# Linear attention and a gated MLP in one kernel: three x sums and two row sums earlier on VectorE, P V one slot sooner

## The chip, the cores and the metric

One NeuronCore of one Trainium2 chip. The time is the device time of one execution in microseconds (us); lower is better.

## The reference

Eight batches of 8 heads, 1024 positions, head size 64. Keys and values are first projected along the sequence to 64 rows, so attention has 64 columns:

```python
k_proj = np.einsum('ks,bhsd->bhkd', E, k)
v_proj = np.einsum('ks,bhsd->bhkd', F, v)
scores = np.matmul(q, k_proj.transpose(0, 1, 3, 2)) / np.sqrt(64)
attn = softmax(scores)                      # over 64 columns
x = concat_heads(np.matmul(attn, v_proj))   # 8192 x 512
out = (silu(x @ w_gate) * (x @ w_val)) @ w_out   # 512 -> 1536 -> 512
```

## The kernel before

**Chunks, tiles, slots.** The 8192 rows are 16 chunks `c` of 512 (batch `b` has chunks 2b and 2b+1, its halves `ch` 0 and 1). The MLP of a chunk runs over 12 tiles `f` of 128 hidden columns, so there are 192 tiles in a row. Each tile `t` is issued in a fixed order: `f_g` (gate matmuls), slot 2t, `f_v` (value matmuls), the tile's "late" list, slot 2t+1. The slots hold the attention of the next batch, so attention and MLP share all engines. `place(b)` puts the steps of batch b's attention in slots counted from `s0 = 48 * (b - 1)`, the first slot of batch b-1's MLP. Slots s0 to s0+23 therefore lie in an even chunk, and s0+24 to s0+47 in an odd one; s0+16 and s0+17 are the two slots of tile 8 of the even chunk, s0+43 and s0+44 the last of tile 9 and the first of tile 10 of the odd one. The order is written out by hand: each engine takes its instructions in the order in which the code issues them, and waits on semaphores for the others.

**Attention steps.** `u_S`: eight score matmuls for two groups (L378), exponential on ACT (L386). `u_R`: row sum and reciprocal on DVE (L408, L409). `u_N`: product with the reciprocal on POOL (L423) and a small running sum `zsum` on POOL (L439). `u_AD`: transposes the products by a DMA. `u_PVt`: eight matmuls of P V into four PSUM banks (L482) and four copies on ACT into `xT` (L491), the MLP's input. The banks are named by letters: `a` (two buffers), `g` (two, shared with the gate's output), `v` (two), `y` and `z` (one each, shared with the output matmuls).

**Pairs of value tiles.** In chunks after the first few, the value product of the tile pairs (2,3), (5,6) and (9,10) is made from seven half-size products instead of eight. For that, sums of blocks of `xT` are needed: `p_x(c, m)` makes them on DVE (L612), for m = 4, 3, 1 and "67", before the pair at tile 2 reads them. They are kept apart for even and odd chunks. `p_34` (first tile of the pair) makes products 4 and 3; `p_1` follows in the same tile's late list; `p_52` is at the second tile, and `p_76` after `f_g` of the tile after the pair. `p_34` takes the next buffer of `v` for its result and holds the other, that of the last `f_v`, for `p_1`; `p_76` adds to a bank that DVE must first have read for `p_52` (`sx`, L632). All matmuls of these have line 621. `gate` (L570) multiplies gate and value into `hT` on DVE; each tile's result waits there until its late list has passed `f_m` and `p_1`.

**The output product** `f_m(c, n)` of a chunk runs in the tiles of the next one, as seven half-size products too (L769). Its inputs `hs` are sums of blocks of `hT`: for m = 5 and 2 on POOL in 12 small steps (`h_sum`, L752, in the late lists of tiles 7, 8 and 11 and of tile 0 of the next chunk), the others on DVE. `f_m` needs m = 5 in tile 2 and m = 2 in tile 3. `m_16` and `m_7` combine the results: L798 and L804 on DVE with L799 on POOL between them. `m_52` copies bank `y` on ACT (L793).

**Late list, chunks after the third.** It is sorted: `f_m` and `p_1` first, then `gate`, then the sums:

```python
todo.sort(key=lambda x: (x[0] not in (f_m, p_1)) * 2)
todo.insert(sum(x[0] in (f_m, p_1) for x in todo), (gate,))
```

Of the kernel before, what the change touches and what calls it, by code (L numbers as in the profile page):

```python
# [26 lines left out]
NFT = DFF // P  # L27
# [16 lines left out]
def kernel(  # L44
# [822 lines left out]
    def put(s, fn, *a):  # L867
        slots[s].append((fn, a))

    def place(b):  # L870
        s0 = 48 * (b - 1)
        if b == 1:
            put(22, u_TD, 1, 0)
            put(29, u_K1, 1)
            put(32, u_KT, 1)
            put(40, u_V1, 1)
            sa = (35, 36, 37, 38, 41, 42, 43, 44)
            put(41, u_AD, 1, 0)
            put(30, u_TD, 1, 1)
            put(47, u_AD, 1, 1)  # L880
            put(46, u_PVt, 1, 0, (0, 1), ("aa", "av"))
        else:
            if b == 2:
                put(s0 + 10, u_KV, b)
            else:
                put(s0 + 8, u_KV, b, "kv", (0, H), "v")
            put(s0 + (13 if b == 2 else 10), u_KT, b)
            put(s0 + (9 if b == 2 else -6), u_TD, b, 0)
            put(s0 + (11 if b == 2 else -4), u_TD, b, 1)
            sa = [s0 + j for j in ((15, 15, 17, 17) if b == 2 else (13, 13, 15, 15)) + (23, 23, 25, 25)]  # L890
            put(s0 + 29, u_AD, b, 0)
            put(s0 + 44, u_AD, b, 1)
            put(s0 + 44, u_PVt, b, 0, (0, 1), ("aa", "yz"))
        for j in range(NJ):
            put(sa[j], u_S, b, j)
            at = sa[j] + 1 if b == 1 else s0 + (
                17, 17 + 2 * (b == 2), 21 if b == 2 else 19, 23 if b == 2 else 21, 35, 37, 41, 42)[j]
            put(at, u_R, b, j)
            put(at, u_N, b, j)
        put(s0 + (68 if b == 1 else 56), u_PVt, b, 1, (0, 1), ("aa", "yz"))  # L900
# [52 lines left out]
    with tc.manual_schedule():  # L953
# [132 lines left out]
        for b in range(1, B):  # L1086
            place(b)
        for b in range(2, B):
            s0 = 48 * (b - 1) - (20 if b == 3 else 24)
# [33 lines left out]
                late[t].append((p_w, m, p))  # L1123
        for c in range(3, NC):
            for i, m in enumerate((4, 3, 1, 67)):
                t = c * NFT + ((-1, -1, 0, 0) if c == 3 else (-3, -3, 0, 1) if c % 2 else (0, 0, 1, 2))[i]
                late[t].append((p_x, c, m))
        for p, cs in PAIRED.items():
            for c in cs:
# [4 lines left out]
        for t in range(NIT):  # L1134
            c, f = divmod(t, NFT)
            ring["wide"] = c < 2
            i = 1 if t < 2 else None
# [46 lines left out]
```

## Time and profile before

| | |
|---|---|
| median of 3 runs | 553.2 us (553.13 to 554.39) |
| profiled execution | 552.91 us, of it a span of 551.4 us from first to last instruction |
| TensorE clock granted | 0.998 of full speed |
| busy, of the span | PE 96%, DVE 78%, POOL 61%, ACT 52% |
| DMA | 62.94 MB, mean 114 GB/s |

PE is TensorE, DVE VectorE, ACT ScalarE, POOL GpSimd; SP issues DMAs. A row of the timeline gives the start in us, the duration, the engine, the line, the operation, what it writes and reads, how many instructions were merged into the row (x4), and in brackets how long the engine had been idle before it and which instruction ended that. A row of the waits gives the waiting engine and line, the one waited for, the total in us, how often, and the longest. A few matmul records are missing, so a group of four may be shown as x3.

### The profile page before, as it was taken

The numbers are of one execution on the slowest core, as the hardware profiler recorded it, in microseconds if no ns is written. First come the engines' busy times: TensorE is split into PE (matmuls) and PEld (weight loads), VectorE is DVE, ScalarE is ACT, GpSimd is POOL, SyncE is SP. The second block draws the span as 40 slices with busy tenths as digits, with TensorE's granted clock in tenths as the row PEclk, the third lists the DMA queues.
The fourth block names the chain that finished last, engine by engine and source line by source line (L and its number), as shares of the span: only waits on it lengthen the run. The fifth ranks groups of instructions, "written<-read, shape, count | busy, mean of one in ns | idle before, by whom it ended". The sixth has DMA issues, their size and how long they took to land.

```text
span 551.4 us, 9977 instructions
## 1 busy us (share of the span) xinstructions
PE 530.6 (96%) x3715; PEld 334.9 (61%) x3780; DVE 431.7 (78%) x724; ACT 288.0 (52%) x515; POOL 333.8 (61%) x428
## 2 busy tenths in 40 slices
PE   8999999999999999999999899998999989999996
PEld 4654545556666666666666666575665756566665
DVE  3787896687788996889887887879978789686874
ACT  3564454573457635566546564566444763453431
POOL 6962494376745957177761878448574574734562
PEclk9999999999999999999999999999999999999999
DMA  9999969829921697009941099314990121200013
GB/s 199 191 196 190 175 142 184 168 76 149 210 63 40 129 214 154 6 36 191 191 115 39 27 196 189 89 39 82 188 198 31 39 77 39 77 35 16 28 40 117
DMA packets 112228, 62.94 MB, mean 114 GB/s; under 512 B 65968, under 2 KB 103856, under 8 KB 112176
## 3 DMA queue, kind: packets, MB, share of 16 engines
q0 software_dynamic: 43952, 29.49, 37.4%
q1 hardware_dynamic: 67392, 31.46, 22.8%
q10 hardware_dynamic: 832, 1.31, 0.8%
q8 instruction: 30, 0.49, 0.3%
q14 instruction: 22, 0.18, 0.1%
HBM read 60.29 MB, written 16.78 MB: 140 GB/s over the span
## 4 chain that ended last, share of the span: by engine, by line
PE 76%; DVE 8%; ACT 6%; POOL 5%; issue 3%; DMA 2%; ACTq 0%; POOLq 0%; DVEq 0%
PE gps L536 23%; PE yps L769 20%; PE vps L536 16%; PE vps L621 9%; DMA wv<-in_moe_w_val_dram 2%; PE kvp L187 2%; PE sc L378 2%; PE yps L703 2%; DVE zr L408 2%; ACT ee L386 2%; POOL AAd L423 1%; POOL hs L752 1%; DVE xsa L612 1%; DVE hT L570 1%; DVE ts L652 1%
## 5 line engine op out<-in xcount | busy, mean ns | idle before, releaser
L536 PE MATMUL gps<-xT,wg 128*128 128x512 bf16 (+1 forms) x729 | 190.9, 377 | 1.7
L752 POOL TENSOR_TENSOR hs<-hT 128x256 bf16<-128x256 bf16 x180 | 130.3, 754 | 29.4 <-DVE hT L570 26.4
L536 PE MATMUL vps<-xT,wv 128*128 128x512 bf16 (+1 forms) x460 | 119.4, 376 | 1.7 <-DMA wv<-in_moe_w_val_dram 0.8
L536 PEld LDWEIGHTS <-wg 128*128 128x128 bf16 x776 | 74.3, 98 | 51.8 <-issue 0.5
L769 PEld LDWEIGHTS <-hs 128*128 128x128 bf16 x900 | 87.5, 98 | 24.7 <-issue 3.1
L799 POOL TENSOR_TENSOR tt<-tt,ysb 128x512 f32<-128x512 f32 x28 | 41.7, 1490 | 85.1 <-DVE tt L798 85.1
L562 ACT ACTIVATE th<-gps 128x512 f32<-128x512 f32 x82 | 49.0, 598 | 78.8 <-PE gps L536 76.0
L423 POOL TENSOR_TENSOR AAd<-ee,zr 128x512 bf16<-128x512 f32 x56 | 59.5, 1062 | 37.1 <-ACT ee L386 17.8
L536 PEld LDWEIGHTS <-wv 128*128 128x128 bf16 x480 | 45.5, 98 | 48.4 <-issue 4.0
L570 DVE TENSOR_TENSOR hT<-th,vps 128x512 bf16<-128x512 f32 x82 | 55.2, 682 | 22.6 <-ACT th L562 13.5
L769 PE MATMUL yps<-ws,hs 128*128 128x256 bf16 x540 | 68.6, 272 | 1.0 <-DVE ysb L838 0.2
L570 DVE TENSOR_TENSOR hT<-thp,sx 128x512 bf16<-128x512 f32 x74 | 58.3, 787 | 3.2 <-DVE sx L632 0.5
L632 DVE TENSOR_TENSOR sx<-ts,vps 128x512 f32<-128x512 f32 x74 | 49.5, 669 | 12.3 <-PE vps L621 10.9
L649 ACT COPY sx<-vps 128x512 f32<-128x512 f32 x37 | 21.7, 586 | 64.6 <-PE vps L621 64.6
L788 POOL TENSOR_TENSOR tt<-xs 128x256 f32<-128x256 f32 x30 | 25.7, 856 | 46.7 <-ACT xs L786 46.5
L769 PE MATMUL yps<-wo,hs 128*128 128x256 bf16 x360 | 48.8, 273 | 0.4 <-ACT xs L786 0.4
L769 PE MATMUL yps<-ws,hT 128*128 128x256 bf16 x360 | 48.8, 273 | 0.4
L752 DVE TENSOR_TENSOR hs<-hT 128x1536 bf16<-128x1536 bf16 (+1 forms) x49 | 46.6, 979 | 0.1
L408 DVE TENSOR_REDUCE zr<-ee 128x8 f32<-128x512 f32 x64 | 42.7, 667 | 3.1 <-ACT ee L386 3.1
L769 PEld LDWEIGHTS <-hT 128*128 128x128 bf16 x360 | 35.2, 98 | 13.2
L612 DVE TENSOR_TENSOR xsa<-xT 128x512 bf16<-128x512 bf16 (+1 forms) x39 | 38.6, 993 | 0.0
L386 ACT ACTIVATE ee<-sc 128x512 f32<-128x512 f32 x64 | 35.5, 597 | 5.3 <-PE sc L378 2.9
(134 smaller groups left out, 729.2 us busy)
## 6 DMA issues: line engine op xcount, KB each, us to landing
out_dram<-ysb SPq DMA_DIRECT2D x27, 512.0 KB, 3.0
qb<-in_q_dram POOLq DMA_DIRECT2D x14, 512.0 KB, 15.4
kb<-in_k_dram POOLq DMA_DIRECT2D x7, 1024.0 KB, 9.7
vb<-in_v_dram POOLq DMA_DIRECT2D x7, 1024.0 KB, 11.4
wo<-in_moe_w_out_dram POOLq DMA_DIRECT2D x2, 768.0 KB, 21.5
out_dram<-ysb SPq DMA_DIRECT2D x6, 256.0 KB, 2.7
kraw<-in_k_dram ACTq DMA_DIRECT2D x2, 512.0 KB, 4.7
qb<-in_q_dram POOLq DMA_DIRECT2D x4, 256.0 KB, 7.9
```

Of the source, the lines that this page charges most:

```text
L386: nc.scalar.activation(out=e[:].rearrange("p h j k -> p (h j k)"), in_=ps[:].rearrange("p a k -> p (a k)"), func=AF.Exp, scale=scale,)
L408: nc.vector.reduce_sum(out=z, in_=e[:], axis=AX.X)
L423: eng.tensor_tensor(out=a.rearrange("p j h k -> p h j k"), in0=ee.pop((b, u))[:], in1=r.unsqueeze(3).to_broadcast([P, 4, 2, KP]), op=ALU.mult,
L536: nc.tensor.matmul(out=ps[:, ts], lhsT=(wg, wv)[w][:, kt, f * P : (f + 1) * P], rhs=x[:, kt, ts], start=(kt == 0), stop=(kt == NKT - 1),)
L562: nc.scalar.activation(out=th[:], in_=ps[:], func=AF.Silu)
L570: nc.vector.tensor_tensor(out=h, in0=th, in1=v, op=ALU.mult)
L612: nc.vector.tensor_tensor(out=sums["x", m, c % 2], in0=i0, in1=i1, op=op)
L621: nc.tensor.matmul(out=ps, lhsT=w[:, kt], rhs=xs[:, kt], start=(start and kt == 0), stop=(kt == 1), skip_group_check=True,)
L632: nc.vector.tensor_tensor(out=out, in0=a.unsqueeze(1).to_broadcast([P, 2, HT]), in1=b, op=op)
L752: eng.tensor_tensor(out=hs[c, m][:, fs, :], in0=quarter(hT[c], *a)[:, fs], in1=quarter(hT[c], *b)[:, fs], op=op,)
L769: nc.tensor.matmul(out=ps, lhsT=lhsT, rhs=ws[m][:, f, :] if rhs is None else rhs, start=(start and f == 0), stop=(f == HF - 1), skip_group ...
L799: nc.gpsimd.tensor_tensor(out=t[:], in0=t[:], in1=yo[c, p][:, 1:3], op=ALU.subtract)
```

## The change

For batches after the second, the row sums and products of groups 0 and 1 go from slot s0+17 to s0+16, so they are issued before `f_v` of tile 8 and ahead of its `gate`. For odd chunks from the fifth on, the x sum m=4 is issued in tile 6 of the chunk before instead of tile 9, m=3 in tile 7 instead of 9, and m=1 in tile 11 of the chunk before instead of tile 0 of its own. P V of a batch's first half (batches from the second on) goes from slot s0+44 to s0+43, ahead of `f_g` of tile 10, and its third bank is a buffer of `g` where it was `y`.

```diff
-            put(s0 + 44, u_PVt, b, 0, (0, 1), ("aa", "yz"))
+            put(s0 + 43, u_PVt, b, 0, (0, 1), ("aa", "gz"))
...
             at = sa[j] + 1 if b == 1 else s0 + (
-                17, 17 + 2 * (b == 2), 21 if b == 2 else 19, 23 if b == 2 else 21, 35, 37, 41, 42)[j]
+                *((17, 19, 21, 23) if b == 2 else (16, 16, 19, 21)), 35, 37, 41, 42)[j]
             put(at, u_R, b, j)
             put(at, u_N, b, j)
...
             for i, m in enumerate((4, 3, 1, 67)):
-                t = c * NFT + ((-1, -1, 0, 0) if c == 3 else (-3, -3, 0, 1) if c % 2 else (0, 0, 1, 2))[i]
+                t = c * NFT + ((-1, -1, 0, 0) if c == 3 else (-6, -5, -1, 1) if c % 2 else (0, 0, 1, 2))[i]
                 late[t].append((p_x, c, m))
```

## The prediction

> **What bounds the kernel now.** I read the page first, then the waits of PE, then the timeline around the longest of them. The page says that PE is the bound and that little of it is idle:
>
> ```profile
> PE 530.6 (96%) x3715; PEld 334.9 (61%) x3780; DVE 431.7 (78%) x724; ACT 288.0 (52%) x515; POOL 333.8 (61%) x428
> ```
>
> The waits of PE, longest first; the second line is the start, and only the first repeats:
>
> ```profile
> PE vps L621 <- DVE sx L632: 7.1, 6, 1.5
> PE warm L992 <- DVE zeros L970: 1.4, 1, 1.4
> ```
>
> Where those waits stand: tiles 8 to 11 of chunk 8 (an even one), 303 to 317 us. To be seen: DVE idles 1.57 us before 305.26, then has no hole until PE waits at 311.62.
>
> ```profile
> 303.00 0.69 DVE L570 TENSOR_TENSOR hT<-thp,sx 128x512 bf16<-128x512 f32 x1
> 303.16 4.20 POOL L752 TENSOR_TENSOR hs<-hT 128x256 bf16<-128x256 bf16 x6
> 305.26 0.69 DVE L570 TENSOR_TENSOR hT<-th,vps 128x512 bf16<-128x512 f32 x1 [1.57 <-ACT th L562]
> 305.87 0.68 DVE L408 TENSOR_REDUCE zr<-ee 128x8 f32<-128x512 f32 x1
> 306.27 0.38 PE L621 MATMUL vps<-xsa,wo 128*128 128x256 bf16 x2
> 307.49 1.15 DVE L652 TENSOR_TENSOR ts<-sx 128x256 f32<-128x256 f32 x1
> 308.56 0.43 DVE L612 TENSOR_TENSOR x<-xT 128x512 bf16<-128x512 bf16 x1
> 308.92 1.26 DVE L612 TENSOR_TENSOR xsa<-xT 128x512 bf16<-128x512 bf16 x1
> 309.10 1.03 PE L536 MATMUL gps<-xT,wg 128*128 128x512 bf16 x3
> 310.93 0.64 DVE L632 TENSOR_TENSOR sx<-ts,vps 128x512 f32<-128x512 f32 x1
> 311.62 0.60 PE L621 MATMUL vps<-xsa,wo 128*128 128x256 bf16 x4 [1.49 <-DVE sx L632]
> 316.57 1.30 POOL L752 TENSOR_TENSOR hs<-hT 128x256 bf16<-128x256 bf16 x2 [0.60 <-DVE hT L570]
> ```
>
> The odd chunk that follows, tile 10 (338 to 342 us): P V, then p_52, then PE at L769 starts late.
>
> ```profile
> 338.63 0.59 ACT L793 COPY ysb<-yps 128x512 f32<-128x512 f32 x1
> 339.29 0.63 PE L482 MATMUL pv<-AT,VS 64*64 64x512 bf16 x8
> 339.39 0.60 ACT L555 ACTIVATE thp<-gps 128x512 f32<-128x512 f32 x1
> 339.85 0.61 PE L621 MATMUL vps<-xT,wo 128*128 128x256 bf16 x4
> 339.96 2.05 ACT L491 CAST xT<-pv 128x512 bf16<-128x512 f32 x4
> 340.60 1.47 PE L769 MATMUL yps<-ws,hs 128*128 128x256 bf16 x12
> ```
>
> A wait is counted from the modelled end of the last matmul, so I count loss by starts. Matmuls of 512 columns start 0.216 us apart and of 256 0.109 apart (the twelve of L769 from 307.79 to 309.10). So p_76 could start at 309.10 + 0.87 = 309.97 and starts at 311.62: **1.65 lost**. The chunks at 180, 377 and 443 us repeat it, the one at 245 loses 0.99 (due 244.49, starts 245.48). Together 7.6 us. At L769 of tile 10 the loss is 340.60 - (339.85 + 0.43) = **0.32**, in six odd chunks, 1.9 us. More than 9.5 us the change cannot take away by these two.
>
> **The change, part by part.** Nothing is added or dropped; instructions change places, no DMA is among them and SP's queue stays. The x sums move in six even chunks, 4 to 14; chunk 14 has no row sums and DVE is busy for 6.5 of 10 us there (500 to 510), so I count nothing for it.
>
> *A. The m=4 sum goes to tile 6.* On the timeline DVE idles 0.70 us before L688 (301.60, waiting for ACT). A sum alone takes 0.43 (308.56), POOL does not run until 302.41. Cost nothing; without that hole the sum would delay p_76 of the pair before by 0.43, and PE's next use of that bank, f_v of tile 8 at 302.80, is 1.6 us later.
>
> *B. The m=3 sum goes to tile 7, two row sums to slot 16.* They now stand on DVE ahead of the tile-8 product L570 (305.26), in the hole of 1.57 us. The sum starts at 303.61. POOL is in its first h_sum until 304.21; rows of L612 beside h_sums took 0.51 and 0.89, alone 0.43, beside the attention product L423 1.26. I take 0.89 (same neighbour, the start falls early in POOL's instruction): 304.50. The two row sums with reciprocals take 1.62 (305.87 to 307.49, L408 to L652). They need only exponentials done at 301.07. L570 starts at about 304.42 + 1.62 = 306.04 instead of 305.26 and ends at 306.73.
>
> The Trainium skill's "SBUF — State Buffer", in "Who interferes with whom", speaks against B: a VectorE instruction with two SBUF inputs and a GpSimd instruction that reads SBUF exclude each other for a whole instruction. By it the sum could take a whole h_sum, 0.67, plus 0.43, so 1.10 as an estimate, and the loss below would be 0.72; the rows of 0.43 to 1.26 agree in kind.
>
> *C. A new wait.* L570 of tile 8 empties the bank that p_1 of tile 9 overwrites (p_34 takes the other bank of v). p_1 starts at 306.27; L570 ended at 305.95, so it had 0.32 to spare. Now it can start at 306.73 + 0.05 (DVE end to PE start, 311.56 to 311.62) = 306.78: **0.51 lost**, and all of f_g(10), p_52, f_m and f_g(11) queue behind it. Bounds: sum of 0.43 gives 0.06, sum of 1.26 gives 0.88. In the chunk at 245 us L691 began 0.35 late, since POOL's L788 came first; there the loss is 0.85.
>
> *D. The p_76 wait goes.* After L570 come ts (0.49 to 1.15, by 307.9), one row sum (0.83, by 308.7) and sx, which needs p_52 (ends 307.96 + 0.51 = 308.5): done 309.4. p_76 is due at 309.97 + 0.51 = 310.48. Gain 1.65 - 0.51 = 1.14 in four chunks, 0.99 - 0.85 = 0.14 in the fifth.
>
> *E. What is late next: POOL.* Two attention products of 1.05 with their zsum (1.37 together) now stand ahead of four h_sums. POOL: first product at 305.4 when its reciprocal ends, second ends with zsum by 308.3, four h_sums (0.67) to 311.0, third product 312.4, L799 (1.27) 313.7, fourth product with zsum 315.2. On DVE L804 waits for L799, then two L570 of 0.69 to 0.91: h_sum f5 starts at about 315.75 instead of 316.57, so 0.8 earlier while PE is 1.14 earlier. The last h_sum that m=5 needs ended at 320.70, PE wanted it at 320.97 (matmuls from 320.53): 0.2 to spare. So 1.14 - 0.8 - 0.2 = 0.14 is given back, more if the m=1 sum, now beside these h_sums, holds up POOL by 0.38 (h_sums of 1.05 for 0.67). Bounds 0 and 0.6; I take **0.25** in four chunks. The m=1 sum at tile 11 is otherwise free (L688 has 0.47 idle before it).
>
> *F. P V a slot sooner, bank g for y.* PE's own order only swaps f_g(10) and P V: p_52 stays due at 339.85 and f_m at 340.28. ACT copies the z bank first; after L793 and L657 it is free at 339.50 and has copied z by 340.0. The 0.32 goes. New conditions: f_g(10) needs silu L651 of tile 9 (ends 338.74; f_g now starts 338.98), f_g(11) needs the g bank copied (340.5; 341.6). L555 now waits behind four copies and ends at 342.0 instead of 340.0; its reader, L570 at 342.52, comes later still. If that cover were gone, DVE would be late by at most 0.2. With y kept, P V would wait for L793 (ends 339.22) at 338.42, 0.8. In the sixth chunk (472 us) PE waits again at 475.09 for a chain through POOL's zsum, so I count five: 1.6 us.
>
> **Sum.** 4 x (1.14 - 0.25) + 0.14 + 1.6 = 5.3 us. The profiled execution took 552.91 (span 551.4 and 1.5 around it), so 547.6; the median of 553.2 stands 0.3 above it: **547.9**.
>
> **Rivals.** *The waits only move* (no gain by D). If the m=3 sum takes 1.26 and L691 is 0.35 late in every chunk, the loss at p_1 is 1.23, and POOL gives back the rest, 0.42. Only F is left: 551.6, with all between that and 549.9. For it: the chunk at 245 us shows that late start once in five; against: POOL runs no L423 at 303.6.
>
> *All goes* (more gain). The sum takes 0.43, p_1 loses 0.06 to 0.2, POOL keeps up: 4 x 1.5 + 0.5 + 1.9 = 8.4, so 544.8. For it: POOL has slept for 6 us before 302.41 and gets its products earlier. Against: the rows of 0.89.
>
> *POOL becomes the bound* (slower). If every h_sum and L799 meets DVE on SBUF (1.05 and 1.58 for 0.67 and 1.27), E's queue frees L799 at 315.5, L804 and two L570 follow, f5 starts at 317.3, and with 4.13 more (316.57 to 320.70; 1.9 on top if all five h_sums take 1.05) m=5's input comes at 321.4 to 323.3: 0.4 to 2.3 after PE wanted it before the change. At 1.2 in five chunks: 6.0 - 1.6 = +4.4, so 557.6. It decides as soon as the f5 h_sum starts after 316.8 on the old scale. Against: only the first of six took 1.05.
>
> **How the numbers follow.** Forecast (545.9 to 549.9) 0.60; all goes 0.17; waits only move 0.14; POOL bound 0.09. The range 545.0 to 551.2 leaves out the slower rival, the ends of the others, some 0.17. 0.3% (1.7 us) is about what a measurement can tell from no change. Faster by over that: 0.60 + 0.17 + 0.09 of the third = 0.86; within: 0.06, the rest of the third and the edge of the slower one; slower: 0.08.
>
> **What would show it.** Right: the wait of L621 on sx falls from 7.1 to below 1; a new one of p_1 (L621) on hT L570 of 0.2 to 0.9, five times; L769 in tile 10 starts 0.43 after p_52; f5 h_sums 0.6 to 1.1 earlier against tile 8. Wrong: p_76 still waits on sx, or PE waits on POOL hs by more than 0.6 in the tile 2 that follows, or f_g(10) or f_g(11) waits on ACT.

## The result, and the profile after

The changed kernel takes 547.73 us (median of 5 runs, 547.3 to 548.0) against 553.53 for the kernel before, run beside it: a ratio of 0.9894, 95% interval 0.988 to 0.9908, so 5.8 us faster. The prediction was 547.9, with 545.0 to 551.2 as its range. The profiled execution took 548.0 us (span 546.5), 4.9 less than that of before.

The two longest waits of PE in the changed kernel (waiting engine and line, the one waited for; us in total, times, longest us):

```profile
PE vps L621 <- DVE sx L632: 1.8, 5, 0.7
PE vps L621 <- DVE hT L570: 1.5, 5, 0.3
```

The 7.1 us on `sx` have become 1.8 (four waits of 0.27 at p_76 of the pair at tile 2, and one of 0.7 near 470 us), and a new wait stands beside them, on L570, five times. The timeline of tiles 7 to 11 of chunk 8 shows where:

```profile
301.75 0.89 DVE L612 TENSOR_TENSOR xsa<-xT 128x512 bf16<-128x512 bf16 x1
...
302.56 0.67 DVE L408 TENSOR_REDUCE zr<-ee 128x8 f32<-128x512 f32 x1
...
303.76 0.82 PE L769 MATMUL yps<-wo,hs 128*128 128x256 bf16 x6
...
304.17 0.65 DVE L570 TENSOR_TENSOR hT<-th,vps 128x512 bf16<-128x512 f32 x1
...
304.74 1.31 DVE L652 TENSOR_TENSOR ts<-sx 128x256 f32<-128x256 f32 x1
304.87 0.38 PE L621 MATMUL vps<-xsa,wo 128*128 128x256 bf16 x2 [0.29 <-DVE hT L570]
...
306.80 0.64 DVE L632 TENSOR_TENSOR sx<-ts,vps 128x512 f32<-128x512 f32 x1
...
307.70 1.03 PE L536 MATMUL gps<-xT,wg 128*128 128x512 bf16 x4
...
308.56 0.60 PE L621 MATMUL vps<-xsa,wo 128*128 128x256 bf16 x4
```

L570 of tile 8 follows the sum and the row sums without its old hole and ends at 304.82; p_1 starts at 304.87. By starts it was due at 304.41 (the six L769 matmuls before it start at 303.76), so it loses 0.46. p_76 at 308.56 follows `f_g` after 0.86 and loses nothing: `sx` was done 1.1 us earlier.

In the odd chunk that follows, P V now stands ahead of `f_g` of tile 10, and L769 follows p_52 after 0.43 without a hole:

```profile
335.70 0.38 PE L621 MATMUL vps<-xsa,wo 128*128 128x256 bf16 x2
336.01 0.63 PE L482 MATMUL pv<-AT,VS 64*64 64x512 bf16 x8
336.57 1.04 PE L536 MATMUL gps<-xT,wg 128*128 128x512 bf16 x4
337.45 0.60 PE L621 MATMUL vps<-xT,wo 128*128 128x256 bf16 x4
337.88 1.47 PE L769 MATMUL yps<-ws,hs 128*128 128x256 bf16 x12
```

What the prediction did not have is in tiles 1 to 4 of that odd chunk. DVE and PE there:

```profile
317.46 1.95 DVE L752 TENSOR_TENSOR hs<-hT 128x1536 bf16<-128x1536 bf16 x1
...
319.33 0.68 DVE L612 TENSOR_TENSOR xsa<-xT 128x1024 bf16<-128x1024 bf16 x1
...
319.93 0.94 DVE L652 TENSOR_TENSOR ts<-sx 128x256 f32<-128x256 f32 x1
...
320.42 1.03 PE L536 MATMUL gps<-xT,wg 128*128 128x512 bf16 x4
...
320.98 0.69 DVE L632 TENSOR_TENSOR sx<-ts,vps 128x512 f32<-128x512 f32 x1
...
321.72 0.60 PE L621 MATMUL vps<-xsa,wp 128*128 128x256 bf16 x4 [0.27 <-DVE sx L632]
```

DVE's own `hs` sum takes 1.95 us (0.95 at 322.38, where POOL runs no sum), and p_76 of the pair at 2 starts at 321.72 where 321.28 was due (`f_g` from 320.42): 0.44 lost, in the four odd chunks from 192 to 387 us.

### The profile page after: what moved, and what is told of

Read it like the earlier page. It is cut to its first block, busy times and chain, and to the rows that moved or that the text cites. A ratio compares the mean times of both kernels' runs of the same rounds, so it can differ in the third digit from the quotient of the medians.

```text
span 546.5 us, 10042 instructions
## 1 busy us (share of the span) xinstructions
PE 533.2 (98%) x3780; PEld 334.3 (61%) x3780; DVE 426.5 (78%) x724; ACT 288.1 (53%) x515; POOL 332.2 (61%) x428
## 4 chain that ended last, share of the span: by engine, by line
PE 72%; DVE 10%; DMA 7%; ACT 5%; POOL 3%; issue 3%; DVEq 0%; ACTq 0%; POOLq 0%
PE gps L536 22%; PE yps L769 20%; PE vps L536 14%; PE vps L621 9%; DMA qTd<-qb 3%; ACT ee L386 2%; PE kvp L187 2%; DVE hT L570 2%; DMA wg<-in_moe_w_gate_dram 2%; DMA kb<-in_k_dram 2%; DVE hs L752 2%; PE sc L378 1%; PE yps L703 1%; PE pv L482 1%; DVE xsa L612 1%
## 5 line engine op out<-in xcount | busy, mean ns | idle before, releaser
L536 PE MATMUL gps<-xT,wg 128*128 128x512 bf16 (+1 forms) x772 | 196.5, 377 | 0.3 <-DMA wg<-in_moe_w_gate_dram 0.3
L752 POOL TENSOR_TENSOR hs<-hT 128x256 bf16<-128x256 bf16 x180 | 131.0, 756 | 29.1 <-DVE hT L570 26.4
L536 PE MATMUL vps<-xT,wv 128*128 128x512 bf16 (+1 forms) x480 | 121.6, 376 | 0.0
L769 PEld LDWEIGHTS <-hs 128*128 128x128 bf16 x900 | 87.3, 98 | 23.6 <-issue 1.2
L799 POOL TENSOR_TENSOR tt<-tt,ysb 128x512 f32<-128x512 f32 x28 | 41.7, 1488 | 83.6 <-DVE tt L798 83.6
L423 POOL TENSOR_TENSOR AAd<-ee,zr 128x512 bf16<-128x512 f32 x56 | 60.7, 1083 | 35.4 <-DVE zr L409 28.6
L570 DVE TENSOR_TENSOR hT<-th,vps 128x512 bf16<-128x512 f32 x82 | 55.1, 680 | 20.8 <-ACT th L562 11.7
L769 PE MATMUL yps<-ws,hs 128*128 128x256 bf16 x540 | 68.6, 273 | 0.2 <-DVE ysb L838 0.2
L570 DVE TENSOR_TENSOR hT<-thp,sx 128x512 bf16<-128x512 f32 x74 | 57.7, 780 | 3.2 <-DVE sx L632 0.5
L752 DVE TENSOR_TENSOR hs<-hT 128x1536 bf16<-128x1536 bf16 (+1 forms) x49 | 49.9, 1045 | 0.1
L769 PE MATMUL yps<-wo,hs 128*128 128x256 bf16 x360 | 49.3, 273 | 0.4 <-ACT xs L786 0.4
L769 PE MATMUL yps<-ws,hT 128*128 128x256 bf16 x360 | 48.8, 273 | 0.0
L769 PEld LDWEIGHTS <-hT 128*128 128x128 bf16 x360 | 35.2, 98 | 13.2
L621 PEld LDWEIGHTS <-wo 128*128 128x128 bf16 x250 | 24.4, 98 | 17.0 <-issue 3.3
```

What stands on the lines that cost most here:

```text
L423: eng.tensor_tensor(out=a.rearrange("p j h k -> p h j k"), in0=ee.pop((b, u))[:], in1=r.unsqueeze(3).to_broadcast([P, 4, 2, KP]), op=ALU.mult,
L536: nc.tensor.matmul(out=ps[:, ts], lhsT=(wg, wv)[w][:, kt, f * P : (f + 1) * P], rhs=x[:, kt, ts], start=(kt == 0), stop=(kt == NKT - 1),)
L570: nc.vector.tensor_tensor(out=h, in0=th, in1=v, op=ALU.mult)
L621: nc.tensor.matmul(out=ps, lhsT=w[:, kt], rhs=xs[:, kt], start=(start and kt == 0), stop=(kt == 1), skip_group_check=True,)
L752: eng.tensor_tensor(out=hs[c, m][:, fs, :], in0=quarter(hT[c], *a)[:, fs], in1=quarter(hT[c], *b)[:, fs], op=op,)
L769: nc.tensor.matmul(out=ps, lhsT=lhsT, rhs=ws[m][:, f, :] if rhs is None else rhs, start=(start and f == 0), stop=(f == HF - 1), skip_group ...
```

## The experiments

Two theories stood at the start. One: each of the two DVE moves is enough to free p_76, and both together push L570 past p_1. The other: one of them does the work and the rest is idle. The losses quoted are by starts, as in the prediction. The first four ran beside a kernel before of 553.37 us, the last four beside one of 552.96.

**e1, the x sums alone.**

```diff
+ x sums of odd chunks: (-6, -5, -1, 1)     # row sums in slot 17, P V in slot 44 as before
```

> Only the x sums are moved; the row sums stay in slot 17 and P V in slot 44. Theory (each move alone empties enough of DVE, the two together overshoot): on the timeline of before the m=3 sum ends at 304.5, inside the hole that ended at 305.26, so L570 of tile 8 keeps its place and p_1 does not wait. Then two row sums to 307.49, ts to 308.64, one row sum to 309.4, sx to 310.05: p_76, due at 309.97, loses 0.1 where it lost 1.65. About 1.0 of this is given back later (in the changed kernel: 0.11 at L769 of tile 2 and 0.44 at p_76 of the pair at 2), so 4 x 1.0 = 4 us faster than before, 549.5. Rival (the row sums are what frees p_76): p_76 still loses over 0.8 in each of five even chunks, gain under 2.5 us, 551 or more.

Measured: 547.36 us, ratio 0.9894 (0.9877 to 0.991), 6.0 faster. p_76 of tile 11 loses nothing and p_1 nothing. At L769 of tile 2 0.19 is given back, and at p_76 of the pair at 2 0.44, in four chunks. So the x sums alone give as much as the whole change. The expected time was too high, by 2.1: I had counted 1.0 in each of four chunks. From one key projection to the next e1 gains 1.26, 0.69, 0.92 and 1.27. The 0.69 is the fifth chunk, at 245 us, which I had left out, and the chunk at 443 us gives nothing back at tiles 2 to 4.

**e2, the row sums alone.**

```diff
+ row sums and products of groups 0 and 1 in slot 16     # x sums and P V as before
```

> Only the row sums of groups 0 and 1 are moved, to slot 16. Theory (each alone is enough): they fill the hole, 303.61 to 305.23, and L570 of tile 8 starts at 305.26 as before, so p_1 does not wait. ts waits for ACT until 306.4, two x sums of 0.43 to 1.26 and a row sum follow to 309.2 to 309.7, sx to 310.3: p_76 loses 0.1 to 0.4 where it lost 1.65; gain 4 x 0.9 = 3.6 us, 549.9. Rival (the x sums are what frees p_76): a loss over 0.8 stays, gain under 2.5 us.

Measured: 545.61 us, ratio 0.9859 (0.9842 to 0.9875), 7.8 faster, so better than the whole change without two of its parts. The timeline of DVE in tiles 8 to 10 of chunk 8:

```profile
302.12 0.63 DVE L408 TENSOR_REDUCE zr<-ee 128x8 f32<-128x512 f32 x1
...
302.95 0.69 DVE L570 TENSOR_TENSOR hT<-th,vps 128x512 bf16<-128x512 f32 x1
304.12 0.86 DVE L652 TENSOR_TENSOR ts<-sx 128x256 f32<-128x256 f32 x1 [0.49 <-ACT sx L649]
...
306.90 0.64 DVE L632 TENSOR_TENSOR sx<-ts,vps 128x512 f32<-128x512 f32 x1
```

L570 ends at 303.64 and p_1 (due and started at 303.96) does not wait; `sx` ends at 307.54 and p_76 starts on time at 307.65. p_76 loses 0.28 in one of the five even chunks and nothing in the others, and the 0.44 of the pair at 2 does not occur; L769 of tile 2 loses 0.19 to 0.25 in four odd chunks. The expected time, 549.9, was too high by 4.3: I had put the gain at 0.9 in each of four chunks, and from one key projection to the next it is 1.79, 0.87, 1.45 and 1.80. Theory one holds for e1 and e2; what the x sums' move gives back was still open.

**e3, P V alone, and e4, P V a slot sooner with bank y.**

```diff
+ put(s0 + 43, u_PVt, b, 0, (0, 1), ("aa", "gz"))     # e3
+ put(s0 + 43, u_PVt, b, 0, (0, 1), ("aa", "yz"))     # e4
```

> Only P V of the first half is moved, one slot sooner with a bank of g. Theory: the 0.31 that L769 lost in tile 10 of six odd chunks goes, p_76 of the even chunks keeps its losses (1.65, 1.65, 1.65, 1.65 and 0.99) and the sixth 0.31 is lost again at 470 to 475 us: 1.6 us faster, 551.9. Rival (the move only shifts the wait to f_g of tile 10 or 11, or to the output products through a later L555): under 0.5 us faster.

> P V one slot sooner, but with bank y as before in place of a bank of g. Theory (the bank is needed for the move): P V wants y at 338.42 and has it only after L793 has copied it, 339.22 plus 0.05: its third product waits 0.5 to 0.8 in six odd chunks, and the 0.31 at L769 goes: 1.2 to 3 us slower than the run with g, 553.5 to 555. Rival (y would have done, the slot alone matters): within 0.5 us of the run with g.

Measured: e3 551.51 us, 0.9966 (0.9954 to 0.9979), 1.9 faster; p_76's losses of 1.65 and 0.99 are all there. e4 554.88 us, 1.0035 (1.0022 to 1.0047), 1.5 slower. A wait that e4 has and the other runs have not:

```profile
PE pv L482 <- ACT ysb L793: 2.6, 6, 0.4
```

P V waits six times for the ACT copy that empties y, 2.6 us in all. From one key projection to the next e4 takes 0.62 more than e3 (66.37 and 65.75 us). The slot alone costs; the bank of `g` makes it a gain.

**e5, the changed kernel with the m=1 sum back in tile 0.**

```diff
- (-6, -5, -1, 1)
+ (-6, -5, 0, 1)
```

> The changed kernel with the m=1 sum put back into tile 0; all else as changed. Theory (the m=1 sum in tile 11 shifts DVE against POOL in tiles 0 and 1, so that DVE's sum hs and the ts after it run behind POOL's instructions, and p_76 of the pair at 2 comes late): the 0.44 lost at p_76 of the pair at 2 in four odd chunks goes, the 0.46 at p_1 in five even chunks stays: 546.0 against 547.7 of the changed kernel. Rival (the 0.44 is lost because PE comes earlier, whichever sums are moved): the 0.44 stays, 547.2 to 548.

Measured: 545.06 us, ratio 0.9859 (0.9843 to 0.9874), 7.9 faster than before, against the changed kernel's 5.8. The 0.46 at p_1 stays in five chunks; the 0.44 is gone, and so are the 0.11 that the changed kernel loses at L769 of tile 2 and the 0.10 that it loses at p_1 of tile 5. Together that is 0.65, and so much less passes from one key projection to the next (64.21 us for 64.86). The same DVE rows as above:

```profile
315.82 1.21 DVE L752 TENSOR_TENSOR hs<-hT 128x1536 bf16<-128x1536 bf16 x1
316.95 1.21 DVE L612 TENSOR_TENSOR xsa<-xT 128x1024 bf16<-128x1024 bf16 x1
318.09 0.41 DVE L652 TENSOR_TENSOR ts<-sx 128x256 f32<-128x256 f32 x1
318.61 0.69 DVE L632 TENSOR_TENSOR sx<-ts,vps 128x512 f32<-128x512 f32 x1
```

From L752's start to the end of `ts` it is 2.68 us where the changed kernel took 3.41. POOL in the two, first the changed kernel, then e5:

```profile
316.04 2.54 POOL L752 TENSOR_TENSOR hs<-hT 128x256 bf16<-128x256 bf16 x4
```

```profile
314.28 3.27 POOL L752 TENSOR_TENSOR hs<-hT 128x256 bf16<-128x256 bf16 x4
```

In the changed kernel POOL's four h_sums run without a gap and DVE's sum waits; in e5 DVE gets in before the fourth of them, which takes 1.38 where it took 0.66. That the m=1 sum in tile 11 makes the loss of 0.44 is shown: it is there in e1, e6 and the changed kernel, which have that sum in tile 11, and in none of the others. How the sum's place does it is not shown; the last section comes back to it.

**e6, the changed kernel with the row sum of group 1 back in slot 17.**

```diff
- (16, 16, 19, 21)
+ (16, 17, 19, 21)
```

> The changed kernel with the row sum of group 1 back in slot 17; that of group 0 stays in slot 16. Theory (p_1 waits because three DVE steps stand ahead of L570 of tile 8): L570 starts 0.83 earlier and ends before p_1 is due, p_1 loses nothing; sx of p_52 is done 0.6 or more before p_76 is due, which loses nothing either: 5 x 0.46 = 2.3 faster than the changed kernel, 545.4. Rival (what is taken from p_1 comes back at p_76 of tile 11, since DVE is full from one to the other): a loss of 0.4 or more there, within 0.6 of 547.7.

Measured: 547.41 us, ratio 0.9901 (0.9886 to 0.9916), 5.5 faster: no better than the changed kernel. The mechanism came out as expected and the time did not. p_1 loses nothing, p_76 of tile 11 loses nothing, and PE now loses 0.55 where the changed kernel lost 0.11, at m=5 of the output product in tile 2:

```profile
317.05 0.60 PE L769 MATMUL yps<-wo,hs 128*128 128x256 bf16 x4
318.04 0.39 PE L769 MATMUL yps<-wo,hs 128*128 128x256 bf16 x2 [0.39 <-POOL hs L752]
```

Neither theory had said this. It is step E of the prediction: once PE comes earlier, POOL's h_sums are late next. The f5 h_sum starts 13.64 us after `f_g` of tile 8, as in the changed kernel (13.65), while PE is 0.46 earlier.

**e7 and e8, the change without one of its DVE moves.**

```diff
+ e7: row sums in slot 16, P V with "gz" in slot 43; x sums as before
+ e8: x sums (-6, -5, 0, 1), P V with "gz" in slot 43; row sums as before
```

> The changed kernel without the x sums' move: row sums at slot 16 and P V a slot sooner with a bank of g. Theory (the x sums' move costs, the other two parts add up): 545.6 of the row sums alone less 1.6 to 1.9 of P V alone: 543.7 to 544.0, and no loss at p_1 nor at p_76 of the pair at 2. Rival (P V's gain depends on the x sums, or the two moves collide on ACT): 545 or more.

> The changed kernel without the row sums' move and with the m=1 sum in tile 0: only the sums m=4 and 3 and P V are moved. Theory (the m=1 sum makes the 0.44, two x sums alone free p_76): x sums alone took 547.4; less 4 x 0.44 and less 1.6 to 1.9 of P V: 543.7 to 544.0. Rival (the 0.44 comes from the order of POOL's h_sums or from PE being early, not from m=1): the 0.44 stays, 545.5 to 545.8.

Measured: e7 544.0 us, ratio 0.9837 (0.9823 to 0.985); e8 542.96 us, ratio 0.982 (0.9807 to 0.9834), 10.0 faster than before. (In e8 the m=1 sum is back in tile 0 as well.) Both have neither the p_1 wait nor the 0.44. e7 came out as expected; e8 is 0.7 below what was expected. e7 keeps 0.2 at m=5 in tile 2 in four chunks and 0.29 at one p_76; e8 loses at most 0.07 at any of these places. No wait of PE that is listed for it comes more than once; the longest, and the one on `sx`:

```profile
PE warm L992 <- DVE zeros L970: 1.4, 1, 1.4
...
PE vps L621 <- DVE sx L632: 0.7, 1, 0.7
```

The 0.7 on `sx` is the one near 470 us, by starts 0.83. e8 beats the changed kernel with two x sums and the P V move alone.

## Why the prediction was right

*Ceiling.* The 7.6 us at p_76 and 1.9 at L769 were the right places, and counting by starts was needed: in the changed kernel the new wait shows as 0.29 and costs 0.46. They were not all the places. By starts the kernel before also loses 0.37 to 0.43 in tiles 2 to 5 of three odd chunks (at 190, 255 and 387 us), where no wait of PE is listed. The ceiling of 9.5 for the two did not count these, and e8, which gains 10.0, loses only 0.06 in each of them.

*A and B.* The m=4 sum took 0.42 in the hole ahead of L688, the m=3 sum 0.89, as taken. The exclusion of DVE and POOL that the Trainium skill's "SBUF — State Buffer" states in "Who interferes with whom" fits in kind, but the estimate of 1.10 from it did not come up there.

*C.* Predicted a loss of 0.51 at p_1, measured 0.46, in all five chunks. For the chunk at 245 us I had 0.85, since L691 started late there; that late start did not recur.

*D.* p_76 of tile 11 loses nothing in any of the five chunks, as worked out. But the sign that went with it, a wait on `sx` below 1 us in all, did not come: it is 1.8, since p_76 of the pair at 2 now waits there.

*E.* Here a term was mis-sized and half of it named wrongly. I took 0.25 per chunk for POOL being late at m=5. Measured: 0.11 there, and 0.44 at p_76 of the pair at 2, so 0.55. I had called the m=1 sum in tile 11 "otherwise free" and feared only that it would hold up POOL. It does, by 0.12: the two h_sums that start at 313.72 take 1.42 where those of e5 (312.09) take 1.30. The dear part came later, at DVE's own `hs` sum, and e5 shows that the m=1 sum in tile 11 costs all of the 0.55. The chain for POOL itself was sound: L804 did wait for L799 (0.95 us), the f5 h_sum came 0.98 earlier against tile 8 where 0.8 was worked out, and e6 shows the m=5 wait as soon as PE is 0.46 earlier.

Not all of the 0.55 is new. In three of these four odd chunks the kernel before already lost 0.27 to 0.33 in tiles 2 to 4. Its m=1 sum, in tile 0, met POOL's h_sums there; the chunk at 186 us:

```profile
186.82 2.34 DVE L612 TENSOR_TENSOR xsa<-xT 128x512 bf16<-128x512 bf16 x1
186.94 2.74 POOL L752 TENSOR_TENSOR hs<-hT 128x256 bf16<-128x256 bf16 x4
```

The sum takes 2.34 to 2.41 in these three chunks, and 0.51 in the fourth, where the kernel before loses nothing (318.36, the row that the prediction used). Its bounds for such a sum, 0.43 to 1.26, left the three out. Against the kernel before, E so cost 0.28, 0.21, 0.65 and 0.27 in the four chunks (the 0.65 with p_1 of tile 5) and nothing in the one at 443 us: 1.4 where the prediction had 1.0.

*F.* The 0.31 is gone in five chunks, 1.6 us on the trace, and e3 alone gained 1.9. The sixth is lost again at p_76 near 470 us (0.84 lost where it was 0.54), as foreseen. Keeping y is dear, but the wait was smaller than I had: 0.8 predicted, 2.6 over six chunks or 0.43 shown in e4, and 0.62 lost in a period against e3.

*The sum.* The periods from one key projection to the next show it: 66.06, 65.48, 65.71 and 66.07 us before, 64.86 each after (64.85 to 64.87), so 3.9 in four periods; the terms of the prediction give 4.1 for them. Over the whole run, C and D brought 5.3 by starts where 4.7 was counted (0.54 for 0.14 in the chunk at 245 us), E cost 1.4 for 1.0, and F brought 1.55 for 1.6. So it is in part luck that 547.9 lies 0.2 from the measured time: the errors in C and in E stand against each other. The start-up was 0.3 slower in the profiled execution (first key projection of batch 2 at 95.60, not 95.34).

*The rivals.* "The waits only move" is in part what happened: 0.46 at p_1 and 0.55 behind it came in place of 1.65. "All goes" was open to the edit, not to this form of it: e8 went past its 544.8 with less moved. "POOL becomes the bound" did not turn the change slower, but its wait is the one that e6 runs into.

## What to carry to other kernels

When an engine's instructions are moved ahead to free a late waiter, ask which earlier waiter stood behind the hole that they fill: a hole of 1.57 us took either 1.62 of row sums or 0.9 of a sum for nothing, and not both. Try the parts of a change one by one: here the whole took 547.7 us, one part alone 545.6, and two parts without the third 544.0. A move that only seems free on its own engine can still make that engine wait for another one two tiles later. And look for lost starts in every chunk, not only where waits are listed: the price of a small sum beside POOL was 0.51 in the chunk that the prediction read and 2.34 in another.

## What the runs showed of the hardware

A DVE sum with two SBUF inputs that meets a queue of POOL sums without gaps waits for two or three of them in a row or for only the rest of one. The 128x1536 sum took 0.95 us with no POOL sum beside it, 1.95 in the changed kernel and 1.21 in e5. The 128x512 sum took 0.41 alone (503.52) and 2.34 beside four POOL sums in the kernel before.

POOL's place in time does not decide it alone. POOL's load of `kb` begins 4.12 us after `f_g` of tile 0 in the changed kernel and 3.99 in e5, but 4.2 in both e1 and e7, and there the same sum took 2.02 and 1.41. What goes with the long wait in these runs is the m=1 sum in tile 11 (1.95 in the changed kernel, 2.02 in e1, 2.39 in e6). In e2, e5, e7 and e8 that sum stands in tile 0, just ahead of POOL's four sums, and the later one took 1.20 to 1.49. Which of the two engines gets in at the end of a POOL instruction, and why, is not settled by these runs.
